# Padded tiles that are filled once, narrower decays on GpSimd, and a last store in two halves

## The chip, the core and the metric

The kernel runs on one core of a Trainium2 chip. The metric is the device time of one execution in microseconds. Engines are named as in the profile: PE is TensorE's matmul row, PEld its weight loads, DVE is VectorE, ACT ScalarE, POOL GpSimd and SP the engine that issues nearly all DMAs; a name with q behind it is the engine's sequencer.

## What is computed

An RWKV attention over 4 batches, 8 heads, 768 steps and a head size of 48, followed by a feed-forward layer of 384 to 1024 to 384 columns with SoLU and a layer norm on 3072 rows. Everything is float32.

```
state = zeros((B, H, D, D))
for t in range(S):
    cur = einsum('bhd,bhe->bhde', u * k_t, v_t)
    y_t = einsum('bhd,bhde->bhe', r_t, state + cur)
    state = w[None, :, :, None] * state + einsum('bhd,bhe->bhde', k_t, v_t)
x = y.transpose(0, 2, 1, 3).reshape(B * S, H * D)
h = x @ w_in
e = exp(h - max(h));  solu = h * e / sum(e)
out = (solu - mean(solu)) / sqrt(var(solu) + 1e-6) * g_ln @ w_out
```

## The kernel before

The sequence is cut into chunks of 128 steps. A batch has six of them, so there are 24 units (batch, chunk), numbered with the batch running fastest; N is 24. Each unit goes through these stages:

- load: SP fetches k and r, 128 steps by 8 heads by 48 columns, into one of five tiles each (kpads, rpads), and v. In these tiles each head has 64 columns; the last 16 are set to zero once by DVE at the start (lines 497 to 499). The 48 columns of a head are runs of 192 bytes in memory.
- decay_k and decay_r (lines 721 to 733): GpSimd multiplies k and r by tables of powers of w (kdec and rdec, which have the same 64 columns for each head) into kp and rp. r is decayed only from unit 9 on; before that TensorE turns the undecayed r. Both products are over all 512 columns of the padded tile.
- weigh (lines 735 to 738): GpSimd multiplies k by u and by r into rku, 384 columns; DVE sums it to own (line 742). diagonal (line 757) puts own on the diagonal of the score matrix, on GpSimd from unit 4 on.
- halve_k, halve_r, turn and join: from unit 9 on ACT or DVE splits kp and rp into 16-bit halves (lines 1145 and 1151), SP has a DMA turn them (line 1119), and DVE joins the turned halves again (line 1124). The normalised rows of the feed-forward layer go the same way (halve_ln and join_ln, with lnT as the result).
- scores, take, outer, merged_y: matmuls of the chunk (lines 822, 916 and 884) with the states between chunks kept inside v's tiles; decay_state (line 959) decays a state on GpSimd.
- ffn_in, unit_a, unit_b, deviation and normalise: the first product of the layer (line 972), exp and SoLU (lines 980 and 1056), the sums for the variance (line 1064) and the scale (lines 1075 to 1088 on GpSimd). From unit 19 on two units at a time are put together out of sums of rows and weights (eleven_a to eleven_d, line 1006).
- ffn_out, or both_a to both_d: the second product (lines 1169 and 1214), the same way in pairs, and the store of the result.

The order of every engine is that in which the code calls these stages; it is written out by hand under manual_schedule, with software lags between the stages (LA = 2 units, LO = 5). One loop runs over the early units, one over units 9 to 17 in pairs (the loop over i that holds the diff's moved lines), one from unit 19 on, and the end is written out. The tile framework adds only the waits between engines. SP issues its DMAs in the order of the code, and each of them waits there for its data.

Tiles of kp and rp come from a rotating pool, five and two of them. In the last six units the rows of the result (rows_out) are put into tiles of kp's pool. The last store is made in both_d: the pair's second unit has its right half of columns stored earlier (line 1277), and its left 192 columns at the end, copied out of PSUM by DVE and stored by SP (lines 1287 and 1288).

direct_path computes all of this and a flag that says whether the inputs lie in the range that it allows. Behind it every engine reads that flag and branches over a general version (lines 1845 to 1847); with the inputs here that version isn't run.

Of the kernel before, what the change touches and what calls it, by code (L numbers as in the profile page):

```python
# [9 lines left out]
F32 = mybir.dt.float32  # L10
# [389 lines left out]
def direct_path(  # L400
# [29 lines left out]
    nc = tc.nc  # L430
    B, H, S, D = r.shape
    T = 128
    P = U = 64
    C = S // T
    HP = H // 2
    dm = H * D
# [5 lines left out]
    SEVEN, EARLY, ON_ACT, ELEVEN = 4, 12, 12, 19  # L442
# [6 lines left out]
    const = ctx.enter_context(tc.tile_pool(name="const", bufs=1))  # L449
    apool = ctx.enter_context(tc.tile_pool(name="apool", bufs=2))  # L450
# [15 lines left out]
    NLD, NV = 5, 6  # L466
    rpads = [const.tile([128, H, P], F32, name=f"rpad{i}") for i in range(NLD)]
    kpads = [const.tile([128, H, P], F32, name=f"kpad{i}") for i in range(NLD)]
    vts = [const.tile([128, 2, H, P], F32, name=f"vt{i}") for i in range(NV)]

    def load(i, which="krv"):
        b, c = units[i]
        for t, src, n in ((kpads, k, "k"), (rpads, r, "r")):
            if n in which:
                nc.sync.dma_start(out=t[i % len(t)][:, :, 0:D],
                                  in_=src[b, :, ts(c, T), :].rearrange("h s d -> s h d"))
        if "v" in which:
            vt = vts[i % NV]
            for n, at, size in ((0, 0, T),) if i < WHOLE else ((0, 0, U), (1, U, U)):
                nc.sync.dma_start(  # L480
                    out=vt[at : at + size, n, :, 0:D],
                    in_=v[b, :, ds(c * T + at, size), :].rearrange("h s d -> s h d"))
# [158 lines left out]
    for vt in vts[:4]:  # L641
        nc.scalar.activation(out=vt[:, 1].rearrange("p h x -> p (h x)"),
                             in_=ident[:, 0:1].to_broadcast([128, H * P]), func=ACT.Copy, scale=0.0)
# [3 lines left out]
    for j in range(8):  # L647
# [5 lines left out]
        else:  # L653
            n = 1 << (j - 1)
# [5 lines left out]
    kdec = const.tile([128, HP, 128], F32, name="kdec")  # L660
    rdec = const.tile([128, HP, 128], F32, name="rdec")
# [17 lines left out]
    N = len(units)  # L679
# [38 lines left out]
        return t[:, 2 * a : 2 * a + 2, :].rearrange("p q d -> p (q d)")  # L718


    def decay_k(i):
        X = live.setdefault(i, {})
        X["kp"] = apool.tile([128, H, P], F32, name="kp", bufs=5)
        nc.gpsimd.tensor_mul(X["kp"].rearrange("p h d -> p (h d)"),  # L724
                             kpads[i % NLD].rearrange("p h d -> p (h d)"),
                             kdec.rearrange("p a d -> p (a d)"))

    def decay_r(i):
        X = live[i]
        X["rp"] = apool.tile([128, H, P], F32, name="rp")  # L730
        nc.gpsimd.tensor_mul(X["rp"].rearrange("p h d -> p (h d)"),  # L731
                             rpads[i % NLD].rearrange("p h d -> p (h d)"),
                             rdec.rearrange("p a d -> p (a d)"))

    def weigh(i, engine, second=None):
        rku = live.setdefault(i, {})["rku"] = apool.tile([128, H, D], F32, name="rku")
# [404 lines left out]
    def halve_k(i):  # L1141
        X = live[i]
        X["both"] = halves()
        parts = X["both"].rearrange("p (o e n) -> p o e n", o=2, e=2)
        nc.scalar.copy(out=parts[:, :, 1], in_=split(X["kp"].rearrange("p h d -> p (h d)")))
# [8 lines left out]
    def halve_rk(i):  # L1154
        if FIRST <= i < N:
            halve_k(i)
            halve_r(i)
# [18 lines left out]
    KH, NH = KF // 2, dm // 2  # L1176
    left, right = slice(0, NH), slice(NH, dm)
# [18 lines left out]
    def turn_next(i):  # L1196
        normalise(i)
        halve_ln(i)
# [20 lines left out]
    def rows_out(i):  # L1219
        if i < N - 6:  # L1220
            return fpool.tile([128, dm], F32, name="o")
        return apool.tile([128, H, P], F32, tag="kp", name="kp",
                          bufs=5).rearrange("p h d -> p (h d)")[:, 0:dm]

    def both_a(i, which=(0, 1, 2)):
        X = live[i]
# [55 lines left out]
    def both_d(i):  # L1282
        X = ending.pop(i)
        (b, c), o2, a = units[i + 1], X["o2"], X["a"]
        rows2 = out[ds(b * S + c * T, T)]
        if i + 2 == N:
            nc.vector.tensor_copy(out=o2[:, left], in_=a)
            nc.sync.dma_start(out=rows2[:, left], in_=o2[:, left])
        else:
            nc.scalar.copy(out=o2[:, left], in_=a)  # L1290
            nc.sync.dma_start(out=rows2, in_=o2)
# [170 lines left out]
    def decay(i):  # L1462
        if i < N:
            decay_k(i)
            decay_r(i)
            weigh(i, nc.gpsimd)

    sum_own(FIRST)
    i = LA + LO
    j, l = i - LA, 0  # L1470
# [41 lines left out]
    for i in range(LA + LO + 2, ELEVEN, 2):  # L1512
        j, l = i - LA, i - LA - LO
        seven = l >= SEVEN
        for n in (i + 6, i + 7):
            if n < N:
                load(n, "kr")
        for n in (i + 3, i + 4):
            if n < N:
                load(n, "v")  # L1520
        deviation(j - 2, j)
        first, second = ([n] if n < N else [] for n in (i + 2, i + 3))
        for n in first + second:
            diagonal(n)
        if SEVEN <= l <= EARLY:
            row_sums_34(l, nc.gpsimd)
        if l < SEVEN:
            decay(i + 4)
        elif i + 4 < N:
            weigh(i + 4, nc.gpsimd)  # L1530
        decay(i + 5)
        if SEVEN <= l + 2 and i + 6 < N:
            decay_k(i + 6)
            decay_r(i + 6)
        ffn_in(j)
        attend([i, i + 1])
        unit_a(j)
        second_pair = i == LA + LO + 2
        if l == EARLY + 4:
            check_next()  # L1540
        if l < EARLY + 4:
            halve_ln(l + 2)
        else:
            normalise(l + 3)
        if seven:
            both_a(l)
        if l == EARLY + 4:
            halve_ln(l + 3)
        for n in (i, i + 1):
            if n < N:  # L1550
                place(n)
        if i >= CHECKED and l < EARLY + 4:
            check_next()
        unit_b(j)
        if l == EARLY + 4:
            deviation(j, j + 1)
        if l <= EARLY:
            normalise(l + 3)
        take([i, i + 1])
        if second_pair:  # L1560
            halve_rk(i + 3)
        if seven:
            take_a(l, "DVE")
        else:
            join_ln(l + 1)
        if l == SEVEN:
            weight_sums((3,))
        check_least()
        if l != SEVEN:
            for n in first:  # L1570
                join_rk(n)
        if second_pair:
            weight_sums((4,))
        if i + 4 < N:
            halve_rk(i + 4)
        if l == EARLY + 4:
            check_next()
        if seven:
            take_a(l, "ACT")
        else:  # L1580
            ffn_out(l)
        if l > EARLY:
            turn_next(l + 3 if l < EARLY + 4 else l + 4)
        ffn_in(j + 1)
        if seven:
            both_b(l)
        unit_a(j + 1)
        if seven:
            both_c(l)
        if l > EARLY:  # L1590
            check_least()
        if l <= EARLY:
            halve_ln(l + 3)
        else:
            turn_next(l + 4 if l < EARLY + 4 else l + 5)
        if l > EARLY:
            check_next()
        if seven:
            both_d(l)
        if l == EARLY + 4:  # L1600
            join_ln(l + 2)
            join_ln(l + 3)
        if i + 4 == ELEVEN:
            input_sums((1, 2), nc.vector)
        for n in (i, i + 1):
            if n < N:
                update(n, i + 2 < ELEVEN)
        for n in first + second if l == SEVEN else second:
            join_rk(n)
        if not seven:  # L1610
            ffn_out(l + 1)
        for n in (i + 4, i + 5):
            if n < N:
                sum_own(n)
        for n in (i, i + 1):
            if n < N:
                merged_y(n)
                take_y(n)
        if i + 2 == ELEVEN:
            eleven_a(j + 2)  # L1620
        if l > EARLY:
            check_least()
        elif i >= CHECKED - 2:
            check_next()
        unit_b(j + 1)
        if l == EARLY + 4:
            deviation(j + 1, j + 2)
        if l <= EARLY:
            normalise(l + 4)
        halve_rk(i + 5)  # L1630
        if l < EARLY + 4:
            join_ln(l + 2)
            if i + 2 == ELEVEN:
                take_first(j + 2)
            if l + 2 >= SEVEN:
                join_ln(l + 3)
        if l + 2 >= SEVEN:
            row_sums_12(l + 2)
        if l + 2 > EARLY:
            row_sums_34(l + 2, nc.vector)  # L1640
        check_least()

    turned = {19: (14, 15), 21: (16, 17), 23: (18,)}
    for i in range(ELEVEN, N - 1, 2):
        j, l = i - LA, i - LA - LO
# [82 lines left out]
    i = N - 1  # L1728
    j, l = i - LA, i - LA - LO
# [148 lines left out]
```

## Time and profile before

| | us |
|---|---|
| median of 3 runs (320.63 to 321.73) | 321.25 |
| the profiled execution, its whole time | 321.01 |
| its span, first to last instruction | 319.3 |
| PE busy in the span | 307.2 |
| DVE busy | 263.9 |
| ACT busy | 246.0 |
| POOL busy | 245.2 |
| TensorE's granted clock, mean | 0.995 of full |

The span begins with the first instruction and ends with the last, the branches behind the result included. The difference between the profiled execution's time and its span lies outside of what the trace shows. The page gives, for each group of instructions, the sum of their times, the mean of one in ns, and the idle time of the engine just before them with the releaser that ended it. Times within the span are given from its start. Busy sums of different engines overlap, and a matmul's end is modelled, so a full PE row means that matmuls follow each other without a gap that the trace can see.

### The profile page before, as it was taken

Reading aid. Unit: us, or ns where it says so; the run is one execution under the profiler, and the core shown is the slowest. Engines: PE = TensorE matmul, PEld = TensorE weight load, DVE = VectorE, ACT = ScalarE, POOL = GpSimd, SP = SyncE. Lnnn points to the kernel's source line nnn. Section 1 sums busy time; section 2 is a strip of 40 time slices with the busy share of each in tenths; the row PEclk is TensorE's granted clock in tenths of the full one; section 3 lists DMA queues with packets and bytes.
Section 4 is the critical chain, followed back from the end, with each engine's and each line's share of the span. In section 5 each row is a group of like instructions: output and inputs, shape, how many; then the busy total and the mean of one; then the engine's idle time right before and its main releaser. Section 6 shows DMA issues by size and latency. Waiting matters only on the chain.

```text
span 319.3 us, 9704 instructions
## 1 busy us (share of the span) xinstructions
PE 307.2 (96%) x3906; PEld 216.1 (68%) x3906; DVE 263.9 (83%) x446; ACT 246.0 (77%) x420; POOL 245.2 (77%) x265
## 2 busy tenths in 40 slices
PE   7999999989999999999999999999999999999991
PEld 5866555555456457678678668668678677769991
DVE  8896999986787979889879799799879946778760
ACT  4877899988569888878968969958969968788420
POOL 5989778899999999999999999989948274273000
PEclk9999999999999999999999999999999999999997
DMA  7999999978999999997998999897867445674912
GB/s 164 247 264 208 204 191 200 118 143 144 192 178 183 181 177 148 167 163 142 170 203 170 189 199 197 175 204 118 141 158 166 77 109 130 145 178 111 218 66 59
DMA packets 165784, 52.64 MB, mean 165 GB/s; under 512 B 158305, under 2 KB 161506, under 8 KB 165730
## 3 DMA queue, kind: packets, MB, share of 16 engines
q1 hardware_dynamic: 165712, 51.92, 83.5%
q8 instruction: 33, 0.54, 0.8%
q14 instruction: 21, 0.17, 0.3%
q10 hardware_dynamic: 18, 0.00, 0.0%
HBM read 26.75 MB, written 4.72 MB: 99 GB/s over the span
## 4 chain that ended last, share of the span: by engine, by line
PE 58%; POOL 16%; DVE 16%; issue 4%; DMA 1%; ACT 1%; SPq 1%; POOLq 0%; ACTq 0%
PE o_ps L1214 26%; PE h_ps L972 15%; PE h_part L1006 8%; POOL rp L731 3%; POOL rku L737 3%; POOL big L757 3%; POOL kp L724 3%; DVE ma L552 2%; PE at L822 2%; PE y_ps L884 2%; POOL rku L738 2%; DVE lnT L1124 2%; DVE big L830 1%; DVE solu L1056 1%; DVE own L742 1%
## 5 line engine op out<-in xcount | busy, mean ns | idle before, releaser
L972 PE MATMUL h_ps<-w_in_sb,xT 128*128 128x512 f32 x216 | 96.9, 598 | 0.0
L972 PEld LDWEIGHTS h_ps<-w_in_sb,xT 128*128 128x128 f32 x216 | 39.9, 190 | 45.0 <-issue 42.7
L1130 ACT COPY halves<-solu 128x2048 uint16<-128x2048 uint16 x23 | 43.6, 1897 | 2.0 <-DMA halves<-halves 1.8
L724 POOL TENSOR_TENSOR kp<-kpad,kdec 128x512 f32<-128x512 f32 x24 | 34.1, 1425 | 2.1 <-DMA kpad<-in_k_dram 0.9
L1124 DVE COPY big<-halves 128x2048 uint16<-128x2048 uint16 x21 | 33.6, 1605 | 1.1 <-DMA halves<-halves 0.8
L1124 DVE COPY lnT<-halves 128x2048 uint16<-128x2048 uint16 x18 | 30.3, 1698 | 0.8 <-DMA halves<-halves 0.8
L738 POOL TENSOR_TENSOR rku<-rku,rpad 128x384 f32<-128x384 f32 x23 | 29.4, 1276 | 1.8
L835 DVE COPY_PREDICATED big<-later_half,at 64x512 f32<-64x512 uint32 x40 | 29.5, 737 | 0.7
L757 POOL TENSOR_SCALAR_AFFINE_SELECT big<-own 64x512 f32<-64x512 f32 x40 | 27.7, 691 | 1.8
L737 POOL TENSOR_TENSOR rku<-kpad,u_bc 128x384 f32<-128x384 f32 x24 | 28.8, 1201 | 0.2
L1214 PE MATMUL o_ps<-w_out_sb,ma 128*128 128x192 f32 x160 | 28.1, 328 | 0.0
L1214 PEld LDWEIGHTS o_ps<-w_out_sb,ma 128*128 128x128 f32 x160 | 26.2, 190 | 1.9 <-issue 1.6
L1064 ACT ACTIVATE e<-solu,stats 128x1024 f32<-128x1024 f32 x20 | 23.0, 1149 | 2.9 <-DVE solu L1056 2.8
L731 POOL TENSOR_TENSOR rp<-rpad,rdec 128x512 f32<-128x512 f32 x15 | 25.1, 1675 | 0.0
L1056 DVE SCALAR_TENSOR_TENSOR solu<-h_ps,stats,e 128x1024 f32<-128x1024 f32 x18 | 23.1, 1283 | 1.5
L980 ACT ACTIVATE e<-h_ps 128x1024 f32<-128x1024 f32 x18 | 18.4, 1023 | 6.4 <-PE h_ps L972 6.1
L1105 ACT ACTIVATE solu<-solu,stats 128x1024 f32<-128x1024 f32 x17 | 21.0, 1234 | 1.1 <-POOL stats L1088 0.9
L1169 PE MATMUL o_ps<-w_out_sb,lnT 128*128 128x384 f32 x64 | 21.5, 489 | 0.0
L1214 PE MATMUL o_ps<-w_out_sb,lnT 128*128 128x192 f32 x112 | 19.8, 330 | 0.7 <-DVE lnT L1124 0.7
L959 POOL TENSOR_TENSOR vt<-vt,wide 48x384 f32<-48x384 f32 x16 | 19.4, 1226 | 0.8
L1214 PEld LDWEIGHTS o_ps<-w_out_sb,lnT 128*128 128x128 f32 x112 | 18.2, 190 | 2.6 <-PE h_part L1006 1.5
L1075 POOL TENSOR_SCALAR stats<-stats 128x2 f32<-128x2 f32 (+2 forms) x13 | 4.7, 365 | 18.8 <-ACT e L1064 18.1
(199 smaller groups left out, 700.0 us busy)
## 6 DMA issues: line engine op xcount, KB each, us to landing
raw<-in_moe_w_out_dram SPq DMA_DIRECT2D x16, 384.0 KB, 4.0
kpad<-in_k_dram SPq DMA_DIRECT2D x24, 192.0 KB, 4.9
rpad<-in_r_dram SPq DMA_DIRECT2D x24, 192.0 KB, 5.1
vt<-in_v_dram SPq DMA_DIRECT2D x40, 96.0 KB, 4.0
raw<-in_moe_w_in_dram SPq DMA_DIRECT2D x7, 512.0 KB, 6.7
out_dram<-o SPq DMA_DIRECT2D x18, 192.0 KB, 3.3
raw<-in_moe_w_in_dram SPq DMA_DIRECT2D x10, 256.0 KB, 3.7
out_dram<-kp SPq DMA_DIRECT2D x5, 192.0 KB, 2.6
```

The costliest lines, as they stand in the source:

```text
L724: nc.gpsimd.tensor_mul(X["kp"].rearrange("p h d -> p (h d)"), kpads[i % NLD].rearrange("p h d -> p (h d)"), kdec.rearrange("p a d -> p (a ...
L731: nc.gpsimd.tensor_mul(X["rp"].rearrange("p h d -> p (h d)"), rpads[i % NLD].rearrange("p h d -> p (h d)"), rdec.rearrange("p a d -> p (a ...
L737: engine.tensor_mul(rku, kpads[i % NLD][:, :, 0:D], u_bc)
L738: (second or engine).tensor_mul(rku, rku, rpads[i % NLD][:, :, 0:D])
L757: nc.gpsimd.affine_select(out=G[rows, c].rearrange("p a q u -> p (a q) u"), in_=X["own"][rows].to_broadcast([U, H, U]), compare_op=ALU.is_ ...
L835: nc.vector.copy_predicated(X["G"][rows, c].rearrange("p a q u -> p q a u"), later_half[rows].unsqueeze(1).to_broadcast([U, 2, HP, U]), X[ ...
L972: nc.tensor.matmul(h_ps[:, ts(n, NX)], X["xT"][:, j, :], w_in_sb[:, j, ts(n, NX)], start=(j == 0), stop=(j == KD - 1))
L1006: nc.tensor.matmul(dst, rows, weights, start=start, stop=True, skip_group_check=True)
L1056: nc.vector.scalar_tensor_tensor(out=solu, in0=X["h"], scalar=rs, in1=X["e"], op0=ALU.mult, op1=ALU.mult, accum_out=tot)
L1124: nc.vector.tensor_copy(out=words.bitcast(U16).rearrange("p n (t o) -> p o n t", o=2), in_=turned)
L1130: copy(out=both.rearrange("p (o n) -> p o n", o=2), in_=split(X["solu"]))
L1214: nc.tensor.matmul(dst, rows[:, f], weights[:, f], start=(start and f == 0), stop=(f == KH - 1), skip_group_check=True)
```

## The change

Five tiles for kp and two for rp are now fixed tiles (kps and rps, chosen by the unit's number), and GpSimd sets their padding to zero once, ahead of the loop. decay_k and decay_r multiply only the 48 columns of each head, so the last 16 keep their zeros. rows_out uses the fixed tiles too. In the loop over the middle units, the calls decay(i + 5), decay_k(i + 6) and decay_r(i + 6) stand behind halve_rk(i + 4) in the code instead of ahead of ffn_in(j). In both_d the last 192 columns are copied and stored as two halves of 96: one by DVE and SP, the other by ACT, which copies it and issues its DMA.

```
+    NK = 5
+    kps = [const.tile([128, H, P], F32, name=f"kp{i}") for i in range(NK)]
+    rps = [const.tile([128, H, P], F32, name=f"rp{i}") for i in range(2)]
...
+    heads = lambda t: t.rearrange("p a (q d) -> p (a q) d", q=2)[:, :, 0:D]
+    for t in kps + rps:
+        nc.gpsimd.memset(t[:, :, D:P], 0.0)
...
     def decay_k(i):
         X = live.setdefault(i, {})
-        X["kp"] = apool.tile([128, H, P], F32, name="kp", bufs=5)
-        nc.gpsimd.tensor_mul(X["kp"].rearrange("p h d -> p (h d)"),
-                             kpads[i % NLD].rearrange("p h d -> p (h d)"),
-                             kdec.rearrange("p a d -> p (a d)"))
+        X["kp"] = kps[i % NK]
+        nc.gpsimd.tensor_mul(X["kp"][:, :, 0:D], kpads[i % NLD][:, :, 0:D], heads(kdec))
 
     def decay_r(i):
         X = live[i]
-        X["rp"] = apool.tile([128, H, P], F32, name="rp")
-        nc.gpsimd.tensor_mul(X["rp"].rearrange("p h d -> p (h d)"),
-                             rpads[i % NLD].rearrange("p h d -> p (h d)"),
-                             rdec.rearrange("p a d -> p (a d)"))
+        X["rp"] = rps[i % 2]
+        nc.gpsimd.tensor_mul(X["rp"][:, :, 0:D], rpads[i % NLD][:, :, 0:D], heads(rdec))
...
     def rows_out(i):
         if i < N - 6:
             return fpool.tile([128, dm], F32, name="o")
-        return apool.tile([128, H, P], F32, tag="kp", name="kp",
-                          bufs=5).rearrange("p h d -> p (h d)")[:, 0:dm]
+        return kps[i % NK].rearrange("p h d -> p (h d)")[:, 0:dm]
...
         if i + 2 == N:
-            nc.vector.tensor_copy(out=o2[:, left], in_=a)
-            nc.sync.dma_start(out=rows2[:, left], in_=o2[:, left])
+            for n, (copy, store) in enumerate(((nc.vector.tensor_copy, nc.sync),
+                                               (nc.scalar.copy, nc.scalar))):
+                part = slice(n * NH // 2, (n + 1) * NH // 2)
+                copy(out=o2[:, part], in_=a[:, part])
+                store.dma_start(out=rows2[:, part], in_=o2[:, part])
...
             weigh(i + 4, nc.gpsimd)
-        decay(i + 5)
-        if SEVEN <= l + 2 and i + 6 < N:
-            decay_k(i + 6)
-            decay_r(i + 6)
         ffn_in(j)
         attend([i, i + 1])
         unit_a(j)
...
         if i + 4 < N:
             halve_rk(i + 4)
+        decay(i + 5)
+        if SEVEN <= l + 2 and i + 6 < N:
+            decay_k(i + 6)
+            decay_r(i + 6)
```

## The prediction

> **What bounds the kernel now.** I read the page from the top, the busy sums and the chain of waits, and then looked for the stretches in which TensorE is not full.
>
> ```profile
> PE 307.2 (96%) x3906; PEld 216.1 (68%) x3906; DVE 263.9 (83%) x446; ACT 246.0 (77%) x420; POOL 245.2 (77%) x265
> ...
> PE 58%; POOL 16%; DVE 16%; issue 4%; DMA 1%; ACT 1%; SPq 1%; POOLq 0%; ACTq 0%
> ```
>
> TensorE is busy for 307.2 of 319.3 us; its idle time is 12.1 us in all. GpSimd carries 16% of the chain of waits, some 51 us, which looks as if every microsecond taken from it were a microsecond won. The chain only says who arrived last at each step, so I asked for the busy times in 8 us stretches (columns: stretch, its length, then busy us and instructions of TensorE, its weight loads, VectorE, ScalarE and GpSimd; granted clock, DMA share, GB/s):
>
> ```profile
> 64.00:72.00 8.00, 7.08 (x140) 4.19 (x140) 6.83 (x13) 6.81 (x12) 7.37 (x7) 1.00 0.78 142
> ...
> 120.00:128.00 8.00, 7.88 (x157) 6.26 (x156) 7.83 (x8) 6.81 (x13) 7.60 (x9) 1.00 0.98 141
> ...
> 208.00:216.00 8.00, 7.33 (x149) 5.04 (x148) 7.72 (x12) 4.78 (x10) 6.92 (x9) 1.00 0.90 207
> ...
> 312.00:319.30 7.30, 0.60 (x4) 0.31 (x2) 0.36 (x1) 0.00 (x0) 0.00 (x0) 0.76 0.23 54
> ```
>
> Between 64 and 208 us, where GpSimd is on the chain and stands at 7.4 to 7.9 of 8, TensorE is at 8.00 in all stretches but two: it misses 0.92 us at 64 to 72 (for ACT's copies, by the waits) and 0.12 at 120 to 128. It misses another 0.67 at 208 to 216, nothing more than 0.23 until 312, and then the tail. So the largest sum that a faster GpSimd can bring between 64 and 312 us is about 1.9 us, whatever it saves for itself.
>
> **The change part by part.** *The multiplications.* The decay rows and the row that is nearest to what they become:
>
> ```profile
> L724 POOL TENSOR_TENSOR kp<-kpad,kdec 128x512 f32<-128x512 f32 x24 | 34.1, 1425 | 2.1 <-DMA kpad<-in_k_dram 0.9
> ...
> L737 POOL TENSOR_TENSOR rku<-kpad,u_bc 128x384 f32<-128x384 f32 x24 | 28.8, 1201 | 0.2
> ...
> L731 POOL TENSOR_TENSOR rp<-rpad,rdec 128x512 f32<-128x512 f32 x15 | 25.1, 1675 | 0.0
> ```
>
> L737 multiplies 384 columns, reading k out of the padded tile in rows of 48 as the new decays will. The means hold waiting; the shortest are 1.27 us for L724 and L731 and 1.00 us for L737 and L738. So each decay gets 0.27 us shorter: 24 and 15 of them, 39 x 0.27 = 10.5 us of GpSimd's 245.2. L959, whose output too lies in padded rows of 48, takes 0.83 us on 48 partitions at its shortest, so rows of 48 in the output aren't dear either; the new form with all three operands in rows isn't in this trace. Its bounds are 0.96 us (the distance at which L737 follows L724) and 1.28 (nothing saved). I take 1.00. A rule speaks against it: the Trainium skill, GPSIMD Engine Reference, section "Performance pitfalls for Q7 kernels", prices a read command that isn't pipelined with the one before at about 102 cycles. If every row of 48 were such a command, two inputs of 8 rows would add, at that page's 1.2 GHz, an estimated 16 x 102 / 1.2 = 1.36 us to each decay, 39 x 1.36 = 53 us in place of the saving, and GpSimd would be the bound. L737 reads 8 such rows and is 1.00 us long, like L738; the row decides, and the rule goes into the low chances.
>
> *What that buys on the path.* From 66.8 to 211.4 us GpSimd has no idle time; 15 kp and 15 rp lie there, 30 x 0.27 = 8.1 us. At 126.2 its lateness (DVE's own waits 1.5 us for rku at 119.07, then two lnT copies and two sums) costs TensorE 0.12 us: six pairs of decays, 3.2 us, come before it, so I count 0.12. The larger place is here:
>
> ```profile
> 210.12 1.29 POOL L731 TENSOR_TENSOR rp<-rpad,rdec 128x512 f32<-128x512 f32 x1
> 210.19 2.41 DVE L1124 COPY big<-halves 128x2048 uint16<-128x2048 uint16 x1
> ...
> 213.41 1.61 DVE L1124 COPY lnT<-halves 128x2048 uint16<-128x2048 uint16 x1
> ...
> 215.16 2.84 PE L1214 MATMUL o_ps<-w_out_sb,lnT 128*128 128x192 f32 x16 [0.68 <-DVE lnT L1124]
> ```
>
> DVE's copy of the turned rows (L1124, at shortest 1.315 us) starts 0.07 us after GpSimd's last rp and takes 2.41: it moves only when rp ends at 211.41. Then come own and the lnT copy, and TensorE, free at 214.48, waits 0.68 us for that. In the changed kernel this rp should be done before 210.19, for which it must be 1.22 us earlier. GpSimd began this turn (L1075) at 192.11 although the sum that it needs from ACT's L1064 was there at 190.13, so a GpSimd that is ahead can start 2.0 us sooner, and the four decays of the turn save 1.1: up to 3.1 us. The copy then takes 1.3, lnT ends at about 213.9, and the 0.68 us are gone. After that no wait of TensorE above 0.23 us is left that could swallow the gain until the tail. Before 66 us nine kp save 2.4 us on GpSimd, but the first chain goes through L737, the diagonals on ACT and DVE's takes, and TensorE's gap at 64 to 67 us is ACT's; I count 0, with 0 to 0.4 as the bounds.
>
> *The memsets.* Seven memsets of 8 rows of 16 columns come behind L713 on GpSimd. Six of the same shape (L623) took 0.93 us together, so 1.09 us, from 4.85 to 5.94. GpSimd then waits for DVE's table until 7.01 (2.16 us idle), which hides them: 0. Without that cover they would cost up to 1.09 us at the start, for L737 at 7.54 follows.
>
> *The move.* Between the old and the new place of decay(i+5) and decay(i+6) in the loop stand TensorE, ACT, DVE and SP instructions (scores, copies, turns, a weight load), and none of GpSimd; the decays issue no DMA. So GpSimd's order stays, and SP's and ACT's too. The new place only names the reader of the fixed tile: rp(15) at 120.22 must wait for halve_r(13), done at 110.83, and rp(17) at 143.46 for halve_r(15), done at 132.89. Being up to 3 us ahead leaves over 6 us of room. Cost 0; if that room were gone, decay, weigh and the state decay behind it would wait on GpSimd, and DVE's own after them.
>
> *The last store.*
>
> ```profile
> 312.64 0.36 DVE L1287 COPY kp<-o_ps 128x192 f32<-128x192 f32 x1 [0.94 <-PE o_ps L1214]
> 313.03 1.09 SPq L1288 DMA_DIRECT2D out_dram<-kp  x1
> ```
>
> Behind the store, every engine branches on the flag (L1846):
>
> ```profile
> L1846 SPq EVENT_SEMAPHORE  x8: 17/17/17, 317.3 to 317.9; - x8
> L1846 ACTq COMPARE_BRANCH  x1: 50/50/50, 310.6 to 310.6; - x1
> ...
> L1846 PEldq COMPARE_BRANCH  x1: 5155/5155/5155, 311.1 to 311.1; - x1
> L1846 ACTq EVENT_SEMAPHORE  x1: 17/17/17, 313.0 to 313.0; - x1
> L1846 DVEq COMPARE_BRANCH  x1: 72/72/72, 313.3 to 313.3; - x1
> ...
> L1846 SPq COMPARE_BRANCH  x1: 58/58/58, 314.5 to 314.5; - x1
> ...
> L1846 DVEq EVENT_SEMAPHORE  x1: 21/21/21, 317.1 to 317.1; - x1
> ```
>
> The copy of 192 columns takes 0.36; by DVE's rows at 192 and 512 columns (0.357 and 0.69) 96 take about 0.26, and ACT's (0.31 at 192, 0.48 at 384) about 0.24: 0.1 us sooner. SP's issue of the last store took 1.09, the two before it 0.33 and 0.34; a half may take 0.33 to 1.09. After its issue SP branches at 314.5 and runs again at 317.3 (the first of its eight events); DVE, whose branch was at 313.3, at 317.1. The data landed 3.7 us after the issue, at 316.7. So SP can win at most 0.86, but DVE (then 317.0) lets only 0.3 through; I take 0.3. Against it stands the DMA page of the Trainium skill (DMA: Bandwidth & Descriptors, section "Specifications"): below 512 B a write is read, modified and written. Rows of 96 columns have 384 B, those of before 768. The page gives no price; loads in rows of 192 B land in 4.0 us for 96 KB here, 0.3 later than this store. The trace makes the halves' landing 316.6, the rule some 316.9, both still behind DVE's 317.0: the sum is the same. ACT now branches after its store too; see the rivals.
>
> *Sum.* 0.68 + 0.12 + 0.3 = 1.1 us. Against the profiled execution (span 319.3, time 321.01, so 1.71 outside) this gives 319.9; on the median of 321.25, which is 0.24 above it, **320.1**.
>
> **The rivals.** *Gaps that stay.* The copy at 210.19 collides with another GpSimd instruction (L1003, which follows), or the tail gives nothing. For it: where GpSimd and DVE meet isn't planned, and L1124, 1.32 us alone, has medians of 1.36 and 1.57 us and reaches 2.41. Against it: L1003 waits for ACT's xT until 212.34. With one of the two, 0.12 to 0.8 us are won: 320.9, or 320.45 at best.
>
> *ACT's late branch (slower).* ACT branched at 310.6 and ran again at 313.0, far ahead of the end. With a store to issue it gets the last sum at 312.62, copies until 312.9, issues for 0.33 to 1.09, reads the flag (0.47) and branches at 313.7 to 314.5. What follows a branch took 2.4 us on ACT, 2.8 on SP, 3.8 on DVE and 5.2 on TensorE. By TensorE's 5.2, ACT is ready at 318.9 to 319.7 instead of SP at 317.3: 1.6 to 2.4 us late, less 0.8 for the gaps: 322.4. It decides from a wait of 2.8 to 3.6 us on ACT. By ACT's own 2.4 it is ready before DVE, or with it; that, and SP's 2.8 at the very time when ACT will branch, speak against it.
>
> *Not what it says.* If the rows of 48 cost what the width saves, decays stay near 1.28 us: only the tail moves, 321.0; by the rule above it would be far slower, and I give that 0.02.
>
> **How the numbers follow.** A measurement of this kernel can tell about 0.3%, 0.96 us, from no change: faster is below 320.29, slower above 322.21. The forecast has 0.53, the gaps that stay and the unchanged decays together 0.27, the late branch and dear rows 0.20 (0.18 and 0.02). With the gap and 0.4 us at the start, 0.3 of the 0.85 us at 64 to 67 and SP's full 0.86 0.68 + 0.12 + 0.4 + 0.3 + 0.86, the best is 318.9; the upper end is taken to the late branch, 322.4. The likeliest case alone has 319.2 to 320.6.
>
> **What would show it.** Right: L724 and L731 at 384 columns with a shortest of about 1.0 us, GpSimd's sum near 235, L1124 at about 210 us near 1.3, TensorE at 8.00 of 8 from 208 to 216, and two stores from SP and ACT with ACT's event at L1846 before DVE's. Wrong: decays at 1.28 or above; a new idle row of GpSimd for halves; a TensorE gap that wasn't there; or ACT as the last to run after its branch.

## The result, and the profile after

In 18 runs of each on one chip the changed kernel took 319.04 us (median; 318.22 to 320.48) and the kernel before 321.02 (319.70 to 322.93): a ratio of 0.9937, with a 95% interval of 0.9919 to 0.9955, or 2.0 us less (1.4 to 2.6). The forecast was 320.1. The profiled execution took 318.6 us, its span is 316.9.

First the page of the changed kernel: busy times, and the chain of waits.

```profile
PE 306.3 (97%) x3906; PEld 216.3 (68%) x3906; DVE 254.6 (80%) x446; ACT 245.4 (77%) x421; POOL 235.6 (74%) x272
...
PE 79%; DVE 8%; ACT 7%; issue 2%; DMA 1%; POOL 1%; POOLq 0%; ACTq 0%; DVEq 0%
```

GpSimd has lost 9.6 us of work and its share of the chain has gone from 16% to 1%; of 51 us on the chain the kernel got 2. VectorE lost 9.3 us too, although not one of its instructions but the last copy has changed. Its 39 copies of turned halves alone took 6.3 us less: 19 of them lasted over 1.5 us before, 11 after. e3_wide below, with wide decays again, has 263.0 us for VectorE.

The decays by line (shortest, median and longest in ns, first and last start in us):

```profile
L732 POOL TENSOR_TENSOR kp<-kpad,kdec x24: 1012/1028/2210, 9.2 to 206.3; 128x384 f32<-128x384 f32 x24
L737 POOL TENSOR_TENSOR rp<-rpad,rdec x15: 1009/1027/2138, 67.2 to 207.2; 128x384 f32<-128x384 f32 x15
```

1.01 us at the shortest for three operands in rows of 48: the value taken from L737 of before (now L741). The rows are not dear, so the prediction's estimate from the rule for unpipelined reads does not apply here. Then the two stretches that the prediction pointed at (columns as there):

```profile
120.00:128.00 8.00, 8.00 (x158) 6.52 (x157) 7.69 (x13) 6.81 (x12) 7.48 (x10) 1.00 0.99 123
208.00:216.00 8.00, 8.00 (x157) 6.25 (x156) 6.56 (x11) 5.09 (x10) 4.38 (x7) 1.00 1.20 220
```

Both are full. The timeline of the second place shows how: the last rp ends at 208.26, before VectorE's copy begins instead of under it, the copy takes 1.37 us instead of 2.41, lnT follows at 211.74 instead of 213.41, and o_ps's matmuls start behind h_part's with no wait.

```profile
207.24 1.02 POOL L737 TENSOR_TENSOR rp<-rpad,rdec 128x384 f32<-128x384 f32 x1
...
209.57 1.37 DVE L1128 COPY big<-halves 128x2048 uint16<-128x2048 uint16 x1
...
211.74 1.32 DVE L1128 COPY lnT<-halves 128x2048 uint16<-128x2048 uint16 x1
...
213.70 2.76 PE L1218 MATMUL o_ps<-w_out_sb,lnT 128*128 128x192 f32 x16
```

At the first place TensorE waited for ma, a sum that VectorE makes out of lnT. Before:

```profile
119.07 0.55 DVE L742 TENSOR_REDUCE own<-rku 128x8 f32<-128x384 f32 x1 [1.52 <-POOL rku L738]
119.54 4.22 DVE L1124 COPY lnT<-halves 128x2048 uint16<-128x2048 uint16 x2
...
125.00 1.20 DVE L1205 TENSOR_TENSOR ma<-ma,lnT 128x512 f32<-128x512 f32 x1
125.74 0.52 POOL L1075 TENSOR_SCALAR stats<-stats 128x2 f32<-128x2 f32 x1
126.35 1.54 PE L1214 MATMUL o_ps<-lows,ma 128*128 128x192 f32 x8
```

After:

```profile
119.92 1.33 DVE L1128 COPY lnT<-halves 128x2048 uint16<-128x2048 uint16 x1 [2.54 <-DMA halves<-halves]
...
120.01 1.28 POOL L1079 TENSOR_SCALAR stats<-stats 128x2 f32<-128x2 f32 x1
...
122.01 0.69 DVE L1209 TENSOR_TENSOR ma<-ma,lnT 128x512 f32<-128x512 f32 x1
...
125.96 1.46 PE L1218 MATMUL o_ps<-lows,ma 128*128 128x192 f32 x8
```

GpSimd reaches the stats 5.7 us sooner. VectorE's 1.52 us of waiting for rku is gone, its lnT copies, 2.1 us each under the decays of before, are down to 1.3 (the one shown even waits for its transfer), and its sums take 0.69 us instead of 1.2. So ma ends at 122.70, 3.3 us ahead of the matmul that reads it; before, it ended at 126.20, 0.15 us ahead. What all that is worth to TensorE is best read from the starts of the same matmul in both traces, since both kernels issue the same 3906 in the same order. Against before, those of after stand at -0.10 us (near 124 us), -0.57 (near 130), -0.62 (211), -1.53 (216), and -1.60 at the end: 0.47 us came at the first place, 0.91 at the second. The granted clock (0.995 before, 0.999 after, over the span) is no rival: between 70 and 300 us and outside the two places the shift moves by no more than 0.05 us.

The tail, from the timeline:

```profile
311.04 0.26 DVE L1294 COPY kp<-o_ps 128x96 f32<-128x96 f32 x1 [0.94 <-PE o_ps L1218]
311.32 0.82 SPq L1295 DMA_DIRECT2D out_dram<-kp  x1
311.33 0.24 ACT L1294 COPY kp<-o_ps 128x96 f32<-128x96 f32 x1 [4.19 <-DVE kp L1294]
311.60 0.39 ACTq L1295 DMA_DIRECT2D out_dram<-kp  x1
```

From PE's end (311.00) to the end of the span 5.86 us pass, against 6.67 before. Read from this pair of profiles alone, the tail had gained 0.8 us, and SP's earlier branch looked like the reason. The expectations of the first experiments say so. It did not hold.

### The profile page after: what moved, and what is told of

Its sections match the earlier page's. It is cut to its first block, busy times and chain, and to the rows that moved or that the text cites. A ratio compares the mean times of both kernels' runs of the same rounds, so it can differ in the third digit from the quotient of the medians.

```text
span 316.9 us, 9715 instructions
## 1 busy us (share of the span) xinstructions
PE 306.3 (97%) x3906; PEld 216.3 (68%) x3906; DVE 254.6 (80%) x446; ACT 245.4 (77%) x421; POOL 235.6 (74%) x272
## 4 chain that ended last, share of the span: by engine, by line
PE 79%; DVE 8%; ACT 7%; issue 2%; DMA 1%; POOL 1%; POOLq 0%; ACTq 0%; DVEq 0%
PE o_ps L1218 27%; PE h_ps L976 23%; PE h_part L1010 9%; PE o_ps L1173 7%; PE y_ps L888 4%; PE at L826 3%; DVE solu L1060 1%; DMA raw<-in_moe_w_out_dram 1%; DVE big L834 1%; PE kv_ps L920 1%; PE h_part L888 1%; ACT e L1072 1%; ACT solu L1071 1%; PE y_ps L865 1%; ACT w_out_sb L571 1%
## 5 line engine op out<-in xcount | busy, mean ns | idle before, releaser
L1128 DVE COPY big<-halves 128x2048 uint16<-128x2048 uint16 x21 | 31.6, 1509 | 1.0 <-DMA halves<-halves 0.7
L761 POOL TENSOR_SCALAR_AFFINE_SELECT big<-own 64x512 f32<-64x512 f32 x40 | 30.1, 753 | 1.8
L1128 DVE COPY lnT<-halves 128x2048 uint16<-128x2048 uint16 x18 | 26.3, 1462 | 5.8 <-DMA halves<-halves 5.8
L741 POOL TENSOR_TENSOR rku<-kpad,u_bc 128x384 f32<-128x384 f32 x24 | 30.5, 1269 | 0.2
L732 POOL TENSOR_TENSOR kp<-kpad,kdec 128x384 f32<-128x384 f32 x24 | 27.6, 1152 | 2.4 <-DMA kpad<-in_k_dram 1.1
L742 POOL TENSOR_TENSOR rku<-rku,rpad 128x384 f32<-128x384 f32 x23 | 24.9, 1084 | 1.8
L963 POOL TENSOR_TENSOR vt<-vt,wide 48x384 f32<-48x384 f32 x16 | 17.7, 1121 | 5.9 <-DVE vt L956 5.4
L1079 POOL TENSOR_SCALAR stats<-stats 128x2 f32<-128x2 f32 (+2 forms) x13 | 5.8, 448 | 21.4 <-ACT e L1068 21.1
L737 POOL TENSOR_TENSOR rp<-rpad,rdec 128x384 f32<-128x384 f32 x15 | 19.5, 1300 | 0.0
```

Source lines behind the costliest of these rows:

```text
L732: nc.gpsimd.tensor_mul(X["kp"][:, :, 0:D], kpads[i % NLD][:, :, 0:D], heads(kdec))
L741: engine.tensor_mul(rku, kpads[i % NLD][:, :, 0:D], u_bc)
L742: (second or engine).tensor_mul(rku, rku, rpads[i % NLD][:, :, 0:D])
L761: nc.gpsimd.affine_select(out=G[rows, c].rearrange("p a q u -> p (a q) u"), in_=X["own"][rows].to_broadcast([U, H, U]), compare_op=ALU.is_ ...
L1128: nc.vector.tensor_copy(out=words.bitcast(U16).rearrange("p n (t o) -> p o n t", o=2), in_=turned)
```

## The experiments

Twelve more runs were made, of eleven new kernels and once more of after, in three groups of four, each group on one chip with the kernel before in between. For each profiled execution the table gives the shift of the same matmul's start against the profile of before: what had gathered by 70 us (the start), what came at the place near 126 us, what came between 211 and 213 us (a stall, see below), what came just behind it at the place near 214 us, then PE's end and what follows it (the tail). The ratio to before is the recorded one, with its interval; it can differ by some 0.001 from that of the two medians.

| kernel | start | 126 us | stall | 214 us | PE's end | tail | ratio |
|---|---|---|---|---|---|---|---|
| before | 0 | 0 | 0 | 0 | 312.61 | 6.67 | 1 |
| after | -0.13 | -0.47 | 0 | -0.91 | 311.00 | 5.86 | 0.9937 (0.9919 to 0.9955) |
| a_again | +0.64 | -0.47 | 0 | -0.91 | 311.79 | 5.74 | 0.9954 (0.9929 to 0.9979) |
| e1_tail | +0.26 | -0.01 | +1.05 | -0.91 | 312.98 | 5.48 | 0.9995 (0.9973 to 1.0018) |
| e2_decays | -0.14 | -0.47 | 0 | -0.91 | 311.16 | 5.22 | 0.9935 (0.9914 to 0.9956) |
| e3_wide | -0.24 | -0.05 | 0 | +0.01 | 312.22 | 6.07 | 0.9985 (0.9964 to 1.0005) |
| e4_one_queue | +0.25 | -0.47 | +0.53 | -0.91 | 311.99 | 5.28 | 0.9947 (0.9926 to 0.9969) |
| e5_late23 | -0.20 | -0.47 | 0 | -0.56 | 311.46 | 5.93 | 0.9961 (0.9941 to 0.9980) |
| e6_late21 | +0.30 | -0.47 | 0 | -0.91 | 311.44 | 5.34 | 0.9960 (0.9936 to 0.9985) |
| e7_early | +1.32 | -0.47 | +1.08 | -0.91 | 313.52 | 5.49 | 0.9971 (0.9951 to 0.9991) |
| e9_late | +0.42 | -0.05 | +0.31 | -0.91 | 312.34 | 5.15 | 0.9968 (0.9944 to 0.9992) |
| g1_pool | +0.85 | -0.47 | 0 | -0.91 | 311.96 | 5.79 | 0.9973 (0.9957 to 0.9989) |
| g2_swap | +3.67 | -0.47 | +1.32 | -0.91 | 316.19 | 5.51 | 1.0075 (1.0050 to 1.0099) |
| g3_both | +2.62 | -0.47 | 0 | -0.91 | 313.80 | 5.80 | 1.0044 (1.0026 to 1.0061) |

### The two halves of the change

e1_tail is the kernel before with the store split:

```
-            nc.vector.tensor_copy(out=o2[:, left], in_=a)
-            nc.sync.dma_start(out=rows2[:, left], in_=o2[:, left])
+            for n, (copy, store) in enumerate(((nc.vector.tensor_copy, nc.sync),
+                                               (nc.scalar.copy, nc.scalar))):
+                part = slice(n * NH // 2, (n + 1) * NH // 2)
+                copy(out=o2[:, part], in_=a[:, part])
+                store.dma_start(out=rows2[:, part], in_=o2[:, part])
```

> The kernel before with only the last store split; the decays stay 512 wide. Theory (narrow decays keep GpSimd out of DVE's way at two places, and the split brings SP's branch forward): PE's last matmul ends where it did before, near 312.6 us in the profile, the rest of the span after it shrinks from 6.7 to 5.9 us, so about 0.7 to 0.8 us faster than before. First rival (the split is worth only the 0.3 us that was predicted and the decays brought the other 1.7): 0.3 us faster, PE end 312.6, tail 6.4. Second rival (ScalarE's late branch costs time): as before or slower.

e2_decays is the kernel after with the same edit backwards.

> The kernel after with the last store whole again, one copy by VectorE and one store by SP. Theory: PE's last matmul ends near 311.0 us, the tail is 6.7 us as before, so 1.5 to 1.6 us faster than the kernel before; the gaps at 126 and 214 us stay closed. First rival (the decays brought 1.7 to 2 us of the gain and the tail little): about 1.7 to 2.0 us faster. Second rival (the gain is the store's alone): no difference to before.

Measured: 0.2 us faster than before for the store alone (by the interval between 0.9 faster and 0.6 slower), 2.1 us for the decays alone (1.4 to 2.8). The decays carry the gain. PE's end in e2_decays, 311.16, is what the theory said. Its tail is not: with the store whole again it should have been 6.7 us and is 5.22, shorter than with the split store of after. The last rows of its timeline say more:

```profile
311.19 0.36 DVE L1291 COPY kp<-o_ps 128x192 f32<-128x192 f32 x1 [0.94 <-PE o_ps L1218]
311.58 2.01 SPq L1292 DMA_DIRECT2D out_dram<-kp  x1
```

SP takes 2.01 us to issue here and branches only at 313.7 (at 312.2 in after), and yet the span ends sooner behind PE. So the time of SP's branch does not set the end. The rows behind the flag, of e2_decays:

```profile
L1850 SPq EVENT_SEMAPHORE  x8: 17/17/17, 314.2 to 315.0; - x8
...
L1850 DVEq COMPARE_BRANCH  x1: 72/72/72, 311.8 to 311.8; - x1
...
L1850 DVEq EVENT_SEMAPHORE  x1: 21/21/21, 315.4 to 315.4; - x1
```

SP runs again half a microsecond after that late branch. What these rows don't show is that SP has eight more such events behind them, at another line. All sixteen take some 1.05 us, and in eight of the 14 profiles the event on GpSimd that gathers all engines follows 0.16 to 0.18 us behind the last of them. In e2_decays they end at 315.5, with VectorE's event at 315.4 just ahead. In after VectorE's event is at 315.4 too, but SP runs again only at 314.9 and is through at 316.0; in before it ran again at 317.3 and was through at 318.4, 1.2 us behind VectorE. From its branch on SP took 2.8 us in before, 2.7 in after, 1.2 in a_again and 0.5 here; why it varies stays open. ScalarE can also be last. In five of the eleven executions in which it issues half of the store, SP's events wait 0.3 to 0.8 us for it, longest in e3_wide, shown here, and g3_both:

```profile
SPq L1880 <- ACTq L1853: 0.8, 1, 0.8
```

In the 13 profiles other than that of before the tail lies between 5.15 and 6.07 us, whole store or split.

### The width alone

e3_wide keeps the fixed tiles, their place in the order and the split store; only the width goes back. The padding is multiplied too, and stays zero.

```
-        nc.gpsimd.tensor_mul(X["kp"][:, :, 0:D], kpads[i % NLD][:, :, 0:D], heads(kdec))
+        nc.gpsimd.tensor_mul(X["kp"].rearrange("p h d -> p (h d)"), kpads[i % NLD].rearrange("p h d -> p (h d)"), kdec.rearrange("p a d -> p (a d)"))
...
```

and the same for rp.

> The kernel after, fixed and once padded tiles and the split store as they are, but all 39 multiplications 512 wide again (the padding is multiplied too). Theory (the width is what matters: 0.27 us for each of 39 instructions): a decay takes 1.27 us again, the PE gaps at 126 and 214 us come back, PE's last matmul ends near 312.6 us, and only the tail's 0.8 us of the gain is left. Rival (the fixed tiles or their place in the order bring it, since a tile from the pool waits for its last reader): PE's end stays near 311.0 us and the kernel is as fast as after.

Both gaps are back, to a few hundredths of a microsecond, and PE ends at 312.22 instead of the expected 312.6, most of which is its earlier start. In its timeline rp again ends under the copy:

```profile
209.83 1.28 POOL L737 TENSOR_TENSOR rp<-rpad,rdec 128x512 f32<-128x512 f32 x1
209.87 2.42 DVE L1128 COPY big<-halves 128x2048 uint16<-128x2048 uint16 x1
...
214.85 1.38 PE L1218 MATMUL o_ps<-w_out_sb,lnT 128*128 128x192 f32 x7 [0.68 <-DVE lnT L1128]
```

What is left is 0.5 us (1.2 faster to 0.2 slower), not told apart from nothing. The fixed tiles and the move together bring nothing that can be told; the width brings 0.47 and 0.91 in these profiles.

### One queue for both halves

e4_one_queue: `(nc.scalar.copy, nc.sync)` in place of `(nc.scalar.copy, nc.scalar)`.

> The kernel after with both halves of the last store issued by SP; the two copies stay on VectorE and ScalarE. Theory (SP's branch sets the end, and a narrower copy and one short issue ahead of it bring it forward): SP issues twice, 0.4 to 0.8 us more ahead of its branch, so the tail is 6.3 to 6.7 us instead of 5.9 and the kernel 0.4 to 0.8 us slower than after. Rival (the split of the copy is what gains, or the landing of the data): the second issue costs nothing that can be seen, tail 5.9.

The theory missed: SP's two issues take 1.54 us together, the tail is 5.28 us, and the median is within the intervals of after. This agrees with what the Trainium skill says on a second issuing engine (DMA: Bandwidth & Descriptors, section "Issuing engines are not separate DMA queues"): it saves sequencer time alone. Here even that time did not count: SP branches 1.9 us behind PE's end instead of 1.2 in after, and yet runs again 3.4 us behind it instead of 3.9.

### GpSimd made late at one unit

e5_late23 repeats rp(23)'s multiplication three times; e6_late21 does the same at rp(21):

```
+        for _ in range(3 if i == 23 else 0):
+            nc.gpsimd.tensor_mul(X["rp"][:, :, 0:D], rpads[i % NLD][:, :, 0:D], heads(rdec))
```

> The kernel after with rp(23)'s decay done four times (three repeats of the same multiplication into the same tile). Theory (at the second place GpSimd's decays of unit 23 run into VectorE's copies of big and lnT[...]): rp(23) now ends near 211.3 us instead of 208.3, the copy that starts near 209.6 is stretched from 1.37 to over 2 us, lnT comes late and o_ps's matmuls start 0.7 to 1 us later: PE's last matmul ends near 311.9 us and about 0.8 us of the gain is lost. Rival (the second gap went for another reason, such as the landing of a transfer): three microseconds more of GpSimd cost nothing there, as GpSimd idles 3.45 us behind rp(23) in any case.

> The kernel after with the same three repeats on rp(21), near 182 us, as a control: as much more work for GpSimd, at a place where it has room. Theory: GpSimd idles for vt and e between there and 209 us, 3 us are swallowed for the most part, no gap opens at 126 or 214 us, time within 0.3 us of after. Rival (any 3 us more on GpSimd cost, as it is the engine behind all others): 0.8 us slower than after or more, as for rp(23).

In e5_late23 the extra decays lie over VectorE's copy, and it is stretched to 2.14 us:

```profile
208.45 4.17 POOL L739 TENSOR_TENSOR rp<-rpad,rdec 128x384 f32<-128x384 f32 x3
209.64 2.14 DVE L1130 COPY big<-halves 128x2048 uint16<-128x2048 uint16 x1
...
212.59 1.31 DVE L1130 COPY lnT<-halves 128x2048 uint16<-128x2048 uint16 x1
214.05 2.19 PE L1220 MATMUL o_ps<-w_out_sb,lnT 128*128 128x192 f32 x12
```

By 216 us TensorE has 0.35 us less of the gain; 0.7 to 1 was expected. Against before, the copy of big is 0.27 us shorter, and lnT's copy, now free of GpSimd, takes 1.31 us instead of 1.61: together the 0.56 us that stay gained. So the mechanism is shown at its place, with half of the price that was expected. The control at unit 21 loses nothing at either place. The two medians don't differ, as 0.35 us is below what they can tell.

This matches the Trainium skill, SBUF — State Buffer, section "Who interferes with whom": VectorE and GpSimd share a pair of ports; a copy in a two-port mode contends for it, and whichever of the two issues first holds it for its whole instruction while the other waits. No run shows which mode the copy is in. The numbers here: 1.37 us alone, 2.14 to 2.42 when a decay started first. The other order stands in e1_tail, whose decays are wide. There VectorE's copy starts 0.29 us ahead of rp(23), and it is rp that is stretched: it takes 2.34 us instead of 1.28.

```profile
210.43 1.53 DVE L1124 COPY big<-halves 128x2048 uint16<-128x2048 uint16 x1
...
212.77 1.47 DVE L1124 COPY lnT<-halves 128x2048 uint16<-128x2048 uint16 x1
```

In before rp(23) was 0.07 us ahead of the copy. So wide decays don't cost the 0.91 us in every execution: in that of e1_tail GpSimd was later still, and the gap was not there.

### Which units count

e7_early uses narrow decays for units up to 15 and the full width behind them; e9_late the other way round.

```
-        nc.gpsimd.tensor_mul(X["kp"][:, :, 0:D], kpads[i % NLD][:, :, 0:D], heads(kdec))
+        if i <= 15:
+            nc.gpsimd.tensor_mul(X["kp"][:, :, 0:D], kpads[i % NLD][:, :, 0:D], heads(kdec))
+        else:
...
```

> Narrow decays for units 0 to 15 alone, full-width ones (128x512, padding included) from unit 16 on. Theory (the first place, at 126 us, is lag that builds up over all decays from 66 us on; the second, at 214 us, is a collision right there): the 0.46 us at 126 us stay gained. From unit 16 on 16 decays take 0.27 us more, 4.3 us, of which GpSimd's new idle takes most; only the four of units 22 and 23 count, so rp(23) ends near 209.3 us instead of 208.3, just before the copy at 209.6: most of the 0.91 us stays gained too, between 0.5 and 0.9. Rival (each place depends on the lag of everything ahead of it): the second gap is fully back, gain 0.46 us in all.

> The other half: full-width decays for units 0 to 15, narrow ones from unit 16 on. Theory: the first gap is back (0.46 us lost), as GpSimd reaches the stats of 126 us 4.5 us late again; from there the 16 narrow decays win back 4.3 us, rp(23) ends near 208.5 us, before the copy of big, and the 0.91 us at 214 us stay gained: about 0.9 us faster than before. Rival (only the total lag matters, GpSimd still behind at 214 us): both gaps back, as before in all but the tail.

The first place follows the early units alone; at the second either half is enough. e7_early keeps the 0.47 us at 126; rp(23) ends at 210.63, before the copy at 211.03, which takes 1.34 us. This execution is 1.3 us later by 70 us, but decay and copy are shifted together.

```profile
209.36 1.27 POOL L743 TENSOR_TENSOR rp<-rpad,rdec 128x512 f32<-128x512 f32 x1
...
211.03 1.34 DVE L1134 COPY big<-halves 128x2048 uint16<-128x2048 uint16 x1
```

In e9_late the first gap is back and the second closed; rp(23) ends at 209.37 and the copy begins at 210.57. The medians are 0.9 us (0.3 to 1.6) and 1.0 us (0.3 to 1.8) faster than before. So the first place depends on the decays up to unit 15 alone. Whether it is the lag that they gather or the collision at the place itself is not shown: kp(15) and rp(15) lie under the lnT copies at 119.5 us and belong to the early units too. In the trace of before both reach ma, the 1.52 us of waiting for rku and about 2.6 us by which copies and sums are longer than in after, and each is more than the 0.47 us lost. The second place is free when rp(23) ends before the copy begins, and in this one execution the lead of the first half survives 16 wide decays, by 0.4 us.

In e7_early's profile the time won at 214 us can't be seen in PE's end, because a stall just ahead of it took 1.08 us. That stall alone would have covered the gap, so the -0.91 of its row in the table proves nothing. The copies do: lnT ends at 214.50, and without the stall o_ps would have started at some 215.2. By the waits of TensorE there:

```profile
PE y_ps L894 <- issue: 0.8, 1, 0.8
```

TensorE waits for nothing that the trace shows. It happened in five of the 14 profiled executions (e1_tail, e4_one_queue, e7_early, e9_late, g2_swap), always before the same matmul. In these five, and in no other, the trace has a 16 KB packet on the instruction queue (q8) that starts 2.4 to 2.7 us before that matmul. In the others the packets lie elsewhere (at 213.6 us in before, at 212.3 in after). So a late code fetch is likely; why it is late in some executions was not settled. The Trainium skill (Runtime: NRT & Kernel Launch, section "Instruction fetch mechanics") says that crossing a 16 KiB block is mostly hidden; if this is such a crossing, it costs 0.3 to 1.3 us where it isn't. In e1_tail the stall costs 1.05 us in place of the gap of 0.91, which that execution would not have had: lnT was ready at 214.24, and without the stall o_ps would have started at some 214.6.

### A second look at after, and an attempt at more

> The kernel after, unaltered, for a second profile and for a comparison on the chip on which the next three run. Theory: GpSimd's lag and the collision are gone in every execution, so against before 0.46 us come at 126 us and 0.91 us at 214 us, less what a late code fetch of PE (a stall of 0.3 to 1.1 us ahead of y_ps's matmul near 212 us in some executions) takes back; with 0 to 0.3 us of the tail 1.4 to 1.7 us faster. Rival (the tail's 0.8 us of the first profile are real): 2.0 to 2.4 us, with a tail of 5.9 us again.

a_again is the kernel after, unaltered: 1.5 us faster than before (0.7 to 2.3), as the two places say, and its tail is 5.74 us. Its start is 0.77 us later than in the first profile of after, all of it before 70 us.

The largest gap left is 1.05 us between 64 and 67 us, of which y_ps waits 0.7 us for ScalarE's copy to big. Two ways to shorten it were tried. g1_pool gives GpSimd four scalings of w_out_sb (L571), two each in two turns of the early loop, which ScalarE did:

```
+            if scalar == 2:
+                nc.gpsimd.tensor_mul(dst, ma.bitcast(F32),
+                                     minus_g[:, f : f + 1].to_broadcast(list(dst.shape)))
...
-            convert_d(p, True)
+            convert_d(p, 2 if i in (4, 5) else True)
```

> The kernel after with the scaling of four weight pieces (w_out_sb from ma and minus_g) moved from ScalarE to GpSimd, which the narrow decays left with room. Theory (PE's gap of 1.05 us between 64 and 67 us is ScalarE's queue): ScalarE is free of two times 0.55 us just ahead, near 51.7 and 59.7 us, and y_ps starts up to 1 us earlier: 0.5 to 1.0 us faster than after. Rival (GpSimd falls behind again by 4 times 1 us and its stats come late at 126 us): the gain at 64 us is given back there, nothing gained.

g2_swap puts ScalarE's copy of tk_ps ahead of its exponential:

```
-            ffn_in(j)
+            ffn_in(j, units=False)
...
         turn_r(i + 2)
         turn_k(i + 2)
+        if i > LA:
+            exponential(j)
```

> The kernel after with ScalarE's order changed in the early loop: the copy of tk_ps to big (0.57 us), on which y_ps waits, ahead of the exponential of h_ps (1.02 us with 0.20 for its sum) instead of behind it. Theory: y_ps starts up to 1.1 us earlier in the gap at 66 us, and 0.6 to 1.0 us are gained by the end. Rival (the exponential then comes 0.6 us late for VectorE's solu, which is next on the path): no gain, or a loss of 0.5 us.

> The kernel after with both: the four scalings on GpSimd and the copy ahead of the exponential. Theory: both shorten the same gap of 1.05 us, so together no more than about 1.1 us, less if one alone closes it. Rival as for the two: GpSimd's lag at 126 us and the late exponential take it back.

None beats after. In g1_pool the gap is still there, now 1.26 us, and another engine holds most of it:

```profile
PE kv_ps L923 <- DVE big L789: 2.5, 2, 1.3
```

VectorE's four conversions ahead of that instruction took 0.52, 0.56, 0.35 and 1.28 us in after, 2.71 together. Now GpSimd's weighing, some 3 us later than in after, lies over them, and they take 4.12:

```profile
61.94 0.64 DVE L553 TENSOR_SCALAR ma<-raw 128x384 uint32<-128x384 uint32 x1
62.62 1.24 DVE L555 SCALAR_TENSOR_TENSOR ma<-raw,ma 128x384 uint32<-128x384 uint32 x1
63.78 0.99 DVE L553 TENSOR_SCALAR ma<-raw 128x384 uint32<-128x384 uint32 x1
64.81 1.25 DVE L555 SCALAR_TENSOR_TENSOR ma<-raw,ma 128x384 uint32<-128x384 uint32 x1
66.09 0.69 DVE L789 TENSOR_TENSOR big<-tr_ps,tab 128x512 f32<-128x512 f32 x1
```

This was on neither side of the expectation: GpSimd does reach the stats near 126 us 3 us later than in a_again, but TensorE loses nothing there (-0.47); it slows VectorE on the spot. In g2_swap the gap does shrink, to 0.37 us, but the kernel is 2.4 us slower than before, where its rival had expected 0.5 at most: the later exponential delays solu, and with it the next h_ps, in four turns:

```profile
PE h_ps L976 <- DVE solu L1060: 4.5, 4, 1.3
```

g3_both shows the same, 1.4 us slower than before. The kernels with all decays narrow and nothing added, after, e2_decays and e4_one_queue, stay the fastest; the runs don't tell them apart.

## Why the prediction was right, step by step

The sign and most of the time came from the right mechanism, narrower decays that leave VectorE alone. Of the terms of the sum, one place was sized right within a quarter of a microsecond, one was nearly four times too small, and the tail stays unproved, with a wrong reading of what limits it.

- *The multiplications.* Predicted 1.00 us each and 10.5 us of GpSimd's work in all; measured 1.01 us at their shortest and 9.6 us. The row nearest to the new form gave it; the 53 us that the prediction estimated for dear rows did not come.
- *The place near 214 us.* The chain of events came as written: rp ends before the copy, the copy takes 1.37 us, lnT ends at 213.06 (predicted 213.9), no wait is left. The size was 0.68 us and is 0.91. e3_wide takes it away, e5_late23 part of it.
- *The place near 126 us.* The size was 0.12 us and is 0.47. This is the step that failed: "At 126.2 its lateness ... costs TensorE 0.12 us". Both sizes were taken from TensorE's visible idle time, and that is a lower bound. At 214 us h_part's modelled end was 2.84 us behind its start, while o_ps's first matmul started 2.68 us behind it in after: 0.16 us of wait lie under a matmul that the trace calls busy. Another 0.08 lies in the o_ps row itself (2.84 us before, 2.76 after). At 126 us the same holds: the rows of o_ps from 123.36 to the next h_ps took 4.36 us, now 4.01, with 0.12 of idle time in sight between them, and 0.11 more lies in the h_ps rows behind. Together the two places gave 1.38 us where 0.80 was counted.
- *The start, the memsets, the move.* Counted at 0. The memsets run in GpSimd's wait as said: the step of 7.01 us is still at 7.01. e3_wide leaves nothing for the move. The start differs by -0.24 to +1.32 us among kernels whose instructions up to 70 us are alike but for the width (g1_pool and the two behind it left out); it is spread between executions.
- *The tail.* Predicted 0.3 us: SP, at 317.3, was taken to be 0.2 us behind VectorE, at 317.1, so that VectorE would soon be the limit. That compared VectorE's event with the first of SP's sixteen; the last came at 318.4, so SP had 1.2 us to give, and in after it is still the last, 0.6 us behind VectorE. VectorE's time from its branch on is no fixed limit either: 3.9 us in before, 3.7 in after, 2.9 in e9_late. The gain can't be proved: 0.2 us for e1_tail, 0.5 for e3_wide, both with intervals over zero, and against e2_decays, which lacks the split, nothing.
- *Sum.* Predicted 1.1 us; the two places and up to 0.3 of the tail give 1.4 to 1.7. The medians gave 2.0 (1.4 to 2.6) and 1.5 (0.7 to 2.3). A stall of 0.3 to 1.3 us in some executions belongs into that and was not foreseen. The predicted 1.1 us lies below the first interval. That it came so near is partly luck: the 0.3 us of the tail, which no run shows, stood in for half of the 0.58 us that the two places brought beyond their 0.80.
- *Rivals.* ScalarE's late branch: ScalarE branches at 312.6 and runs again at 315.6, 3.0 us later and 0.2 us after VectorE. That is the lower end of the 2.8 to 3.6 us from which this rival decides, and short of TensorE's 5.0. In this execution it costs nothing, as SP's events go on until 316.0. In e3_wide ScalarE took 3.6 us and SP waited 0.8 for it: the rival is real there, though smaller than its 1.6 to 2.4 us:

```profile
L1853 ACTq COMPARE_BRANCH  x1: 54/54/54, 312.6 to 312.6; - x1
...
L1853 DVEq EVENT_SEMAPHORE  x1: 21/21/21, 315.4 to 315.4; - x1
L1853 ACTq EVENT_SEMAPHORE  x1: 17/17/17, 315.6 to 315.6; - x1
```

  Gaps that stay, and decays that stay wide in time, fell with the timeline. Another new wait did appear: ScalarE's half copy starts only when VectorE's ends ("4.19 <-DVE kp L1294"), so the two copies run one behind the other, where the prediction had them side by side.

## What to carry to other kernels

Work taken from an engine that never rests counts only where the engine that sets the end waits for it; here 9.6 us of GpSimd made 1.4 us for TensorE, in two places that a table of busy times by stretches shows beforehand. Size such a place by the starts of the same matmul in two traces, or take the visible idle time as a lower bound. Don't read a tail of a few microseconds from one pair of profiles: over 14 executions it varied by 1.5 us, with no link to how the store was split. And look at who starts first where two engines collide: a third of a microsecond decided here which of them waited.

## What was not expected of the hardware

- VectorE's copy of 128x2048 halves takes 1.37 us beside an idle GpSimd and 2.14 to 2.42 us under a decay. When the copy starts 0.29 us first, it takes 1.53 us and the decay 2.34. Narrower GpSimd work so gave VectorE 9.3 us back, all but 0.1 of it without a change to it.
- The issue of one DMA by SP at the end took between 0.40 us (e3_wide) and 2.25 us (a_again), and the 2.01 us of e2_decays sit in the second shortest tail.
- TensorE stalls of 0.3 to 1.3 us before one and the same matmul in five of 14 executions, each with a packet on the instruction queue 2.4 to 2.7 us ahead.
- What follows the branch on the flag took 0.5 to 2.8 us on SP, 2.5 to 3.6 on ScalarE and 2.9 to 3.9 on VectorE in the 14 executions.
